# One SBUF region for all loaded tiles, one run a partition for the weights, and V loaded in pairs

## Chip, cores, metric

The kernel runs on one core of one Trainium2 chip. A time is the device time of one execution, in microseconds (us); the smaller, the better. Of a kernel run several times the median is given. The profile is one further execution, recorded by the hardware profiler.

## The reference

One decoding step of a transformer block for 4 sequences (B = 4, D = 576), bfloat16 inputs. An attention with 32 query heads over 16 cached key/value heads (window of 2,048 positions, head width 128) and a mixer with an MLP (F = 4,608) run side by side on the same normed input, and both are added to x:

```python
xn = _layernorm(x)
# attention
q = (xn @ wq)                                   # 4 x 4096, 32 heads
k, v = k_cache[:, :, Sk - W:], v_cache[:, :, Sk - W:]   # W = 2048, each head serves 2 query heads
p = softmax(q k^T * Dh ** -0.5)
a = (p v) @ wo
# mixer and MLP on xn (sequence length 1: the shifted parts are all zeros, so hs = 0)
x1 = xn + hs
h2 = gelu(_layernorm(x1) @ w3) @ w4
out = x + a + x1 + h2
```

The bytes are K and V, 33.6 MB each, wq and wo, 4.7 MB each, w3 and w4, 5.3 MB each: 87 MB read once, for 4 tokens.

## The kernel before

**Loads.** All large loads are issued by SyncE (the SP queue), in the order in which the program names them; a load whose buffer is still in use holds up those behind it. Four buffers of 32 KB a partition (pool `big`, `NBUF = 4`) take K and V in tiles of 4.2 MB: 8 tiles of K, then 8 of V, K0 to K7 and V0 to V7. Each K or V tile has 128 rows of 32,768 contiguous bytes, one to a partition: 32 heads, four quarters of 512 positions. The weights share these buffers. wq comes as four rows a partition (`wq`, 32 KB) and a tail of 64 rows (`wq_t`, in a `kt` buffer); w3 as two rows a partition twice (`w3a`, `w3b`) and a tail; wo as two tiles of 16 rows (`wo0` in a buffer of its own, `wo1`); w4, which is 2 halves of 18 rows a partition, as 11 rows in what is left of the buffer of `w3b`, and after V as 7 + 7 rows in one DMA, 6, 3, and two last rows in two halves of columns (`w_end`). The order of the queue is wq, K0, w3a, K1, w3b with 11 rows of w4, K2 to K7, V0 to V7, wo0, wo1, w_end.

**K stage.** `k_scores(n)` takes a K tile: DVE transposes it in four pieces (L301), PE multiplies the pieces with the queries (L310) and gathers the scores in PSUM banks S. For K5 to K7 DVE also takes the maximum of a bank in between (L287). After K0 and K1 PE runs `g_piece` (L486), xn times w3; after K1 `gelu()` follows on DVE, ACT and PE, and the first 11 rows of w4 are multiplied.

**Between K and V.** The maximum over all scores, four exponentials on ACT (L352), `pick_rows` (8 matmuls, L363) which spreads the probabilities over partitions, `keep_rows` (L368), then `spread_rows(n)`, four DVE operations for each V tile (L381), which writes the weights X.

**V stage.** `v_compute(n)` is 64 matmuls of 128 x 256 (L394). The order of PE, ACT and DVE is that of the program from here on (`manual_schedule`). After V1 PE picks rows for the second half of the heads and turns the reciprocals; after V3 ACT scales the first half (`heads_out(0)`); after V4 `heads_rows(0)` and `heads_pick(0)`, matmuls OX (L424) and three DVE steps (L429 to L433), turn it into the columns `onx` that wo is multiplied with. `v_load(n + 3)` is issued after `v_compute(n)`, when the buffer of V(n - 1) is free.

**The end.** After V7: `heads_out(1)`, `heads_rows(1)`, `heads_pick(1)`, 64 matmuls with wo (`acc_matmuls`, L441), the rest of w4 (`mlp_out`), the sums (`copy_sums`, `merge_sums`), and the last rows of w4 in quarters of columns (`quads`, L455), whose two output copies go to HBM.

Small pieces of SBUF come from `Z`, a tile of 16 KB a partition, through `z_part`.

Of the kernel before, what the change touches and what calls it, by code (L numbers as in the profile page):

```python
# [9 lines left out]
ALU = mybir.AluOpType  # L10
# [5 lines left out]

NBUF = 4
# [3 lines left out]
def kernel(  # L21
# [32 lines left out]
    KJ = 4  # L54
# [3 lines left out]
    DH = D // 2  # L58
    scale = float(Dh) ** -0.5
# [22 lines left out]
    big = ctx.enter_context(tc.tile_pool(name="big", bufs=NBUF))  # L82
    ktp = ctx.enter_context(tc.tile_pool(name="kt", bufs=2))
    pzp = ctx.enter_context(tc.tile_pool(name="pz", bufs=1))
    wop = ctx.enter_context(tc.tile_pool(name="wo", bufs=1))
# [13 lines left out]
    def k_load(bp, kq):  # L99

        t = big.tile([P, CK, Dh], BF16, tag="big", name=f"k{bp}{kq}")
        lo = Sk - W + kq * 4 * CK
        src = k_rows[MT * bp:MT * bp + MT, lo:lo + 4 * CK, :].rearrange("m (q c) d -> m q (c d)", q=4)
        nc.sync.dma_start(out=t[:].rearrange("p c d -> p (c d)"), in_=src)
        return t
# [3 lines left out]
    def v_load(n):  # L109
        bp, kq = V_order[n]  # L110
        t = big.tile([P, CK, Dh], BF16, tag="big", name=f"v{n}")
        lo = Sk - W + kq * 4 * CK
        src = v_rows[MT * bp:MT * bp + MT, lo:lo + 4 * CK, :].rearrange("m (q c) d -> m q (c d)", q=4)
        nc.sync.dma_start(out=t[:].rearrange("p c d -> p (c d)"), in_=src)
        return t

    wq_src = A_wq[0:KJ * P, :].rearrange("(p j) n -> p j n", j=KJ)
    w3_src = B_w3[0:KJ * P, :].rearrange("(p j) f -> p j f", j=KJ)
    w4_src = B_w4.rearrange("(e m i) n -> e m i n", e=2, i=NFH)
    NE0 = 11  # L120
    w4_row = w4_src[0, :, NE0:NFH, :].rearrange("m i n -> m (i n)")
    w4_both = bass.AP(w4_row.tensor, w4_row.offset, [list(w4_row.ap[0]), [(P * NFH - NE0) * D, 2], list(w4_row.ap[1])])
    XR = 16
    NT = Hq * Dh // (P * XR)
    wo_src = A_wo.rearrange("(t p x) n -> p t (x n)", p=P, x=XR)

    JR = 2

    def load_rows(t, a, src, j, n, rows=JR):

        nc.sync.dma_start(out=t[:, a:a + rows * n].rearrange("p (j n) -> p j n", j=rows), in_=src[:, j:j + rows, :])
        return [t[:, a + i * n:a + (i + 1) * n] for i in range(rows)]

    def load_tail(t, a, w, n):
        nc.sync.dma_start(out=t[:, a:a + n // 2], in_=w[KJ * P:D, :].rearrange("r (e f) -> (r e) f", e=2))
        return t[:, a:a + n // 2]

    BIG = CK * Dh


    wq_t = load_tail(ktp.tile([P, NQ // 2], BF16, tag="kt", name="wq_t"), 0, A_wq, NQ)
    wq_m = big.tile([P, BIG], BF16, tag="big", name="wq")
    wq_j = load_rows(wq_m, 0, wq_src, 0, NQ, KJ)
    K_order = [(bp, kq) for bp in range(2) for kq in range(4)]
    V_order = K_order
    K_tiles = {0: k_load(*K_order[0])}
# [26 lines left out]
    def transposed_prep(src_bf, name, pad=0):  # L173
        dup = const.tile([B, 2, P], BF16, name=f"dup_{name}")
        nc.vector.memset(dup[:], 0.0)
        for e in range(2):
            nc.vector.tensor_copy(out=dup[:, e, e:P:2], in_=src_bf[:, KJ * P:D])
        T = const.tile([P, KJ + 2, B + 2 * pad], BF16, name=name)
        if pad:
            nc.vector.memset(T[:], 0.0)  # L180
        return src_bf, dup, T[:, :, pad:pad + B], T

    def transposed_pe(prep):
        src_bf, dup, T, _ = prep
        tp = ps_tp.tile([P, KJ + 2, B], BF16, tag="tp")
        for j in range(KJ):
            nc.tensor.transpose(out=tp[:, j, :], in_=src_bf[:, j:KJ * P:KJ], identity=ident[0:B, 0:B])
        for e in range(2):
            nc.tensor.transpose(out=tp[:, KJ + e, :], in_=dup[:, e, :], identity=ident[0:B, 0:B])
        nc.vector.tensor_copy(out=T, in_=tp[:])  # L190

# [10 lines left out]

    qz = z_part(2 * NM * NY * G, BF16).rearrange("p (a m y n) -> p a m y n", a=2, m=NM, y=NY)

    layernorm(xn_f, xn_bf, x_bf)
    xn_prep = transposed_prep(xn_bf, "xnT", B)
    xnT = xn_prep[3]
# [8 lines left out]
    GP0 = 320  # L218
# [4 lines left out]
    HB = QN // Dh  # L223
    qp = ps_s.tile([P, QN], F32, tag="S", name="qp")
    nc.vector.memset(qp[:], 0.0)
    transposed_pe(xn_prep)

    def q_piece(t, j):
        for n in range(NQ // QN):
            i, k = divmod(n, 2)  # L230
            if j < KJ:
                x, rhs = xnT[:, j, :], t[:, n * QN:(n + 1) * QN]
            else:
                e, f0 = divmod(n * QN, NQ // 2)
                x, rhs = xnT[:, KJ + e, :], t[:, f0:f0 + QN]

            nc.tensor.matmul(out=qp[32 * i:32 * i + 2 * B, :], lhsT=x[:, B - B * k:3 * B - B * k], rhs=rhs,  # L237
                             start=False, stop=False, skip_group_check=True)

    q_piece(wq_t, KJ)  # L240
    for j in range(KJ):
        q_piece(wq_j[j], j)
# [10 lines left out]

    tq = ps_o.tile([P, 2, HB // rep, NY, rep, 4 * B], F32, tag="O", name="tq")
    rows = bass.AP(ident[:].tensor, ident[:].offset, [list(ident[:].ap[0]), [B, 2], [G, 4], [1, B]])
    for y in range(NY):
        for m in range(HB):
            m2, r = divmod(m, rep)
            nc.tensor.matmul(out=tq[:, :, m2, y, r, :].rearrange("p k (i b) -> p k i b", b=B),
                             lhsT=q_rows[:, m, y, :, :].rearrange("p g i -> p (g i)"), rhs=rows,  # L260
                             start=(y + m == 0), stop=(y == NY - 1 and m == HB - 1), skip_group_check=True)
    YM = NY * G
    for g in range(NG):
        g1, g0 = divmod(g, 2)
        for bp in range(2):
            src = ap_part(tq, G * g, G, 2 * g0 * B + 2 * bp + g1,
                          [[rep * 4 * B, 4 * NY], [B, 2], [4 * B, rep]])
            dst = ap_part(qz, G * g, G, bp * NM * YM + 8 * g0 + 4 * bp + 2 * g1,
                          [[G, 4 * NY], [4 * YM + 16, 2], [1, rep]])
            if bp:  # L270
                nc.scalar.copy(out=dst, in_=src)
            else:
                nc.vector.tensor_copy(out=dst, in_=src)
# [3 lines left out]
    ln2T = ln2_prep[2]  # L277
# [11 lines left out]
    def k_scores(n):  # L289

        bp, kq = K_order[n]
        kn = K_tiles.pop(n)
# [31 lines left out]
    sums = z_part(DH, F32)  # L324

# [32 lines left out]
    def pick_rows(bp, g0, g1):  # L358
        for r in range(rep):
            if (bp, r) not in CPS:  # L360
                CPS[bp, r] = ps_s.tile([P, NG * CK], F32, tag="S", name=f"C{bp}{r}")
            for q in range(4):
                nc.tensor.matmul(out=CPS[bp, r][:, g0 * CK:g1 * CK], lhsT=pick[:, bp, r, 3 - q:3 - q + P],  # L363
                                 rhs=EP[:, g0:g1, q, :], start=(q == 0), stop=(q == 3), skip_group_check=True)
# [81 lines left out]
    def load_wo(t, pool, tag):  # L446
        w = pool.tile([P, XR, D], BF16, tag=tag, name=f"wo{t}")
        nc.sync.dma_start(out=w[:].rearrange("p x n -> p (x n)"), in_=wo_src[:, t, :])
        return w

# [18 lines left out]
    NI3 = NFH // 2  # L469
    G_banks = []  # L470

    def g_open():
        for k in range(2):
            bank = ps_o.tile([P, 4 * P], F32, tag="O", name=f"G{k}")
            nc.vector.memset(bank[:], 0.0)
            G_banks.append((bank[:], 4 * k, 4))
        G_banks.append((ACC[:, GP0:GP0 + P], 8, 1))

    def g_piece(t, j):
        w = t if len(t.shape) == 2 else t[:]  # L480
        for bank, i0, n in G_banks:
            for a in range(4):
                e, h = divmod(a, 2)
                lhsT, f0 = (ln2T[:, j, :], e * (F // 2)) if j < KJ else (ln2T[:, KJ + e, :], 0)
                rhs = bass.AP(w.tensor, w.offset + f0 + NI3 * h + i0, [list(w.ap[0]), [1, n], [NFH, P]])
                nc.tensor.matmul(out=bank[32 * a:32 * a + B].rearrange("p (i m) -> p i m", m=P), lhsT=lhsT, rhs=rhs,  # L486
                                 start=False, stop=False, skip_group_check=True)

    def gelu():
        z_at[0] = 2 * NM * NY * G  # L490
        xs = z_part(NI3 * P, F32)
        u = z_part(NI3 * P, F32)
        g = z_part(NI3 * P, BF16)
        for k, (bank, i0, n) in enumerate(G_banks):
            (nc.scalar.copy if k == 1 else nc.vector.tensor_copy)(out=xs[:, i0 * P:(i0 + n) * P], in_=bank)
        nc.vector.tensor_tensor(out=u, in0=xs, in1=xs, op=ALU.mult)
        nc.vector.tensor_scalar(out=u, in0=u, scalar1=GA, scalar2=1.0, op0=ALU.mult, op1=ALU.add)
        nc.vector.tensor_tensor(out=u, in0=u, in1=xs, op=ALU.mult)
        nc.scalar.activation(out=u, in_=u, func=ACT.Tanh, scale=GC)
        nc.vector.tensor_scalar(out=u, in0=u, scalar1=0.5, scalar2=0.5, op0=ALU.mult, op1=ALU.add)  # L500
        nc.vector.tensor_tensor(out=g, in0=u, in1=xs, op=ALU.mult)  # L501
        GT = ps_tp.tile([P, NI3, 4, B], F32, tag="tp", name="GT")
        cols = bass.AP(ident[:].tensor, ident[:].offset, [list(ident[:].ap[0]), [32, 4], [1, B]])
        for i in range(NI3):
# [155 lines left out]
```

## Time and profile before

| | us |
|---|---|
| median of 3 runs | 212.45 |
| the runs | 211.96, 212.45, 212.47 |
| the profiled execution's own time | 211.72 |
| its span in the profile | 209.8 |
| busy in it: PE / DVE / ACT | 120.4 / 134.9 / 15.2 |
| transfers of the SP queue, as a share of 16 DMA engines' span | 97.3% |
| HBM read | 87.17 MB, 416 GB/s over the span |

The span runs from the first to the last instruction; what the program needs around it, 1.9 us here, is in the time alone. PE, PEld (weight loads), DVE (VectorE), ACT (ScalarE) and POOL (GpSimd) are the compute engines, SPq is the queue of SyncE, which issues the loads. Lines such as L394 are those of the kernel's source as printed above. "Idle before" names the wait that ended last before an instruction. A window's line gives its bounds, its length, the busy time of each engine with the number of instructions, the share of TensorE's clock that was granted (PEclk), the share in which the 16 DMA engines were busy, and GB/s. The trace also holds a record for each DMA packet, that is one contiguous run of one partition.

### The profile page before, as it was taken

Reading aid. Unit: us, or ns where it says so; the run is one execution under the profiler, and the core shown is the slowest. Engines: PE = TensorE matmul, PEld = TensorE weight load, DVE = VectorE, ACT = ScalarE, POOL = GpSimd, SP = SyncE. Lnnn points to the kernel's source line nnn. Section 1 sums busy time; section 2 is a strip of 40 time slices with the busy share of each in tenths; the row PEclk is TensorE's granted clock in tenths of the full one; section 3 lists DMA queues with packets and bytes.
Section 4 is the critical chain, followed back from the end, with each engine's and each line's share of the span. In section 5 each row is a group of like instructions: output and inputs, shape, how many; then the busy total and the mean of one; then the engine's idle time right before and its main releaser. Section 6 shows DMA issues by size and latency. Waiting matters only on the chain.

```text
span 209.8 us, 2498 instructions
## 1 busy us (share of the span) xinstructions
PE 120.4 (57%) x1096; PEld 74.9 (36%) x1096; DVE 134.9 (64%) x137; ACT 15.2 (7%) x40; POOL 1.8 (1%) x8
## 2 busy tenths in 40 slices
PE   1434069019145333334444426999799999959562
PEld 0111012002021111111111002887688898848441
DVE  7904792098689898989999614996626848700202
ACT  4002100000200000000000053000200100000101
POOL 2100000000000000000000000000000000000000
PEclk9999557856955555555555555899999999988998
DMA  7999899999999999999999999999999999999992
GB/s 301 400 469 431 381 481 397 424 418 473 439 400 447 437 412 406 481 412 406 472 419 400 469 425 406 462 422 412 456 422 419 444 428 425 409 422 429 411 404 78
DMA packets 4593, 87.31 MB, mean 416 GB/s; under 512 B 476, under 2 KB 1000, under 8 KB 1768
## 3 DMA queue, kind: packets, MB, share of 16 engines
q1 hardware_dynamic: 4568, 87.17, 97.3%
q8 instruction: 8, 0.13, 0.3%
q10 hardware_dynamic: 16, 0.01, 0.0%
q14 instruction: 1, 0.01, 0.0%
HBM read 87.17 MB, written 0.00 MB: 416 GB/s over the span
## 4 chain that ended last, share of the span: by engine, by line
DMA 54%; PE 29%; DVE 11%; ACT 2%; issue 2%; SPq 1%; DVEq 0%; ACTq 0%
DMA k<-in_A_k_cache_dram 41%; PE O L394 21%; DMA w_end<-in_B_w_dram 13%; DVE kt L301 10%; PE G L486 3%; PE C L363 3%; PE S L310 2%; ACT Z L352 1%; DVE mx L287 1%; DVE X L381 1%; ACT Z L368 0%; PE OX L424 0%; SPq L512 0%; PE ACC L486 0%; PE RD L407 0%
## 5 line engine op out<-in xcount | busy, mean ns | idle before, releaser
L301 DVE STREAM_TRANSPOSE kt<-k 128x2048 int32<-128x2048 int32 x32 | 71.4, 2283 | 12.5 <-DMA k<-in_A_k_cache_dram 12.5
L394 PE MATMUL O<-v,X 128*128 128x256 bf16 x512 | 59.5, 281 | 3.9 <-DMA v<-in_A_v_cache_dram 2.3
L310 PE MATMUL S<-kt,Z 128*32 128x512 bf16 x256 | 28.7, 592 | 51.1 <-DVE kt L301 51.1
L394 PEld LDWEIGHTS <-X 128*128 128x128 bf16 x512 | 51.5, 101 | 12.3 <-DVE X L381 2.6
L381 DVE TENSOR_TENSOR X<-Z,own 128x1024 int32<-128x1024 int32 x32 | 37.0, 1220 | 17.9 <-ACT Z L368 6.9
L310 PEld LDWEIGHTS <-Z 128*32 128x32 bf16 x256 | 9.9, 125 | 70.0 <-issue 67.5
L429 DVE TENSOR_TENSOR Z<-OX,own_d 128x512 f32<-128x512 f32 x2 | 1.4, 692 | 18.7 <-PE OX L424 18.7
L363 PE MATMUL C<-Z,pick 128*128 128x512 bf16 x16 | 5.5, 502 | 4.1 <-ACT Z L352 4.1
L352 ACT ACTIVATE Z<-S,nb 128x512 bf16<-128x512 f32 x4 | 2.7, 692 | 64.2 <-DVE nb L562 64.2
L252 DVE CAST q_rows<-qp 128x256 bf16<-128x256 f32 x4 | 1.5, 420 | 7.2 <-PE qp L237 6.5
L486 PE MATMUL G<-w3a,ln2T 128*4 128x512 bf16 x24 | 6.1, 1087 | 0.0
L237 PE MATMUL qp<-wq,xnT 128*8 128x512 bf16 x32 | 3.3, 584 | 3.6 <-DMA wq<-in_A_wq_dram 3.6
L416 ACT ACTIVATE Z<-O,rd_rows 64x128 f32<-64x128 f32 x4 | 1.4, 362 | 46.1 <-PE O L394 46.0
L486 PEld LDWEIGHTS <-ln2T 128*4 128x4 bf16 x60 | 2.1, 107 | 6.8 <-issue 6.4
L363 PEld LDWEIGHTS <-pick 128*128 128x128 bf16 x16 | 1.9, 117 | 7.3 <-issue 6.5
L460 DVE COPY Z<-ACC 64x288 f32<-64x288 f32 x1 | 0.5, 460 | 6.2 <-PE ACC L441 6.2
L505 PE MATMUL GT<-ident,Z 128*128 128x16 bf16 x9 | 0.4, 176 | 7.0 <-DVE Z L501 7.0
L368 ACT CAST Z<-C 128x128 bf16<-128x128 f32 (+2 forms) x6 | 3.0, 544 | 19.7 <-PE C L363 19.7
L486 PE MATMUL G<-w3b,ln2T 128*4 128x512 bf16 x16 | 4.1, 1093 | 0.0
L287 DVE TENSOR_REDUCE mx<-S 128x1 f32<-128x512 f32 x4 | 2.6, 662 | 2.0 <-PE S L310 2.0
L441 PEld LDWEIGHTS <-gT 128*4 128x4 bf16 x62 | 2.3, 96 | 4.4 <-issue 2.6
L237 PEld LDWEIGHTS <-xnT 128*8 128x8 bf16 x40 | 1.2, 111 | 5.7 <-issue 5.3
(95 smaller groups left out, 56.6 us busy)
## 6 DMA issues: line engine op xcount, KB each, us to landing
k<-in_A_k_cache_dram SPq DMA_DIRECT2D x8, 4096.0 KB, 28.7
v<-in_A_v_cache_dram SPq DMA_DIRECT2D x8, 4096.0 KB, 22.0
wo<-in_A_wo_dram SPq DMA_DIRECT2D x2, 2304.0 KB
wq<-in_A_wq_dram SPq DMA_DIRECT2D x1, 4096.0 KB, 12.6
w3a<-in_B_w_dram SPq DMA_DIRECT2D x1, 2304.0 KB, 26.8
w3b<-in_B_w_dram SPq DMA_DIRECT2D x1, 2304.0 KB
w_end<-in_B_w_dram SPq DMA_DIRECT2D x1, 2016.0 KB, 25.1
w3b<-in_B_w_dram SPq DMA_DIRECT2D x1, 1584.0 KB
```

The source lines that it names most:

```text
L237: nc.tensor.matmul(out=qp[32 * i:32 * i + 2 * B, :], lhsT=x[:, B - B * k:3 * B - B * k], rhs=rhs, start=False, stop=False, skip_group_chec ...
L252: nc.vector.tensor_copy(out=dst, in_=src)
L287: nc.vector.reduce_max(out=mx[:, g:g + 1], in_=S[g][:], axis=AX.X)
L301: nc.vector.transpose(out=ap32(kt[e], c0 * 2 * G, [[2 * G, C2 // 2], [1, 2], [2, G]]), in_=ap32(kn, c0 * 4 * G + e * G, [[4 * G, C2 // 2], ...
L310: nc.tensor.matmul(out=S[kq][c:c + 32, :].rearrange("p (c q l) -> p c q l", q=4, l=2), lhsT=qz[:, bp, m, y, :], rhs=kt[e][:, :, 4 * m:4 * ...
L352: nc.scalar.activation(out=EP[:, g].rearrange("p q (c l) -> p c q l", l=2), in_=S[g][:].rearrange("p (c q l) -> p c q l", q=4, l=2), func= ...
L363: nc.tensor.matmul(out=CPS[bp, r][:, g0 * CK:g1 * CK], lhsT=pick[:, bp, r, 3 - q:3 - q + P], rhs=EP[:, g0:g1, q, :], start=(q == 0), stop= ...
L368: nc.scalar.copy(out=CB[:, bp, g0:g1, :, r], in_=CPS[bp, r][:, g0 * CK:g1 * CK].rearrange("p (g c) -> p g c", c=CK))
L381: nc.vector.tensor_tensor(out=ap32(X, a * CX * MT, [[MT, CX], [1, MT]]), in0=bass.AP(s32.tensor, s32.offset, [list(s32.ap[0]), [1, CX], [0 ...
L394: nc.tensor.matmul(out=O_tiles[bp][:], lhsT=X[:, c:c + 2, :].rearrange("p c n -> p (c n)"), rhs=vn[:, c:c + 2, :].rearrange("p c d -> p (c ...
L441: nc.tensor.matmul(out=ACCS[half][o0:o0 + B, 0:DH], lhsT=lhsT, rhs=row[:, q * DH:(q + 1) * DH], start=False, stop=False, skip_group_check= ...
L486: nc.tensor.matmul(out=bank[32 * a:32 * a + B].rearrange("p (i m) -> p i m", m=P), lhsT=lhsT, rhs=rhs, start=False, stop=False, skip_group ...
```

## The change

- One region `ring` of 144,000 bytes a partition replaces the buffers of `big` and `wo`. It has four slots of 32 KB, between the second and the third a gap of 64 elements. K tile n lies in slot n mod 4. Loads wait for whoever reads or writes the bytes that they overwrite.
- wq, w3 and wo are loaded as they lie in HBM, cut into 128 equal runs: 36,864, 41,472 and 36,864 bytes a partition, nine half rows of wq and w3, 32 rows of wo. wq and w3 go to slots 2 and 3 and past them, and both are issued ahead of K0.
- Because a partition now holds half rows, the normed input is transposed into nine slots, each with two groups of columns (`transposed_prep`, `transposed_pe`, `slot_cols`), 20 transposes for 12; q takes 36 matmuls of 512 columns for 40, w3 (`g_all`) 36 of 512 and 18 of 128 for 40 and 20, in one go ahead of the scores of K0.
- V is loaded two tiles at a time, 65,536 bytes a partition, into slots 0 and 1 or 2 and 3: `v_load(0)` and `v_load(2)` ahead of the V stage, `v_load(4)` after V1, `v_load(6)` after V3. `pick_rows` reads the probabilities in the order that goes with it.
- All of w4 comes after V: a half of 18 rows (`w4_e0`), and after wo 7, 6, 3 and the two last rows. The first half and wo lie in slots 0 and 1; 6, 3 and 2 rows lie past slot 3.
- wo in one run makes `XR` 32 and `NT` 1: `heads_rows` has 2 products for 4, and the three DVE steps of `heads_pick` have half the columns.
- GELU: two copies to SBUF on ACT after `g_all`; then, on 640 columns for 1,152, two DVE passes and the tanh after V4, one DVE pass and 5 matmuls for 9 after V5 (`gelu_u`, `gelu_g`, `gelu_T`).
- Some DVE memsets become matmuls with zeros or go to POOL.

The core of the diff:

```diff
-    wq_t = load_tail(ktp.tile([P, NQ // 2], BF16, tag="kt", name="wq_t"), 0, A_wq, NQ)
-    wq_m = big.tile([P, BIG], BF16, tag="big", name="wq")
-    wq_j = load_rows(wq_m, 0, wq_src, 0, NQ, KJ)
-    K_tiles = {0: k_load(*K_order[0])}
+    E1 = (7, 6, 3, 2)
+    GAP = max(0, wo_n + E0_N + E1[0] * D - 2 * TILE)
+    SLOT = [0, TILE, 2 * TILE + GAP, 3 * TILE + GAP]
+    REST = SLOT[3] + TILE
+    ring = ringp.tile([P, RING], BF16, tag="ring", name="ring")
+    def load_run(t, src):
+        nc.sync.dma_start(out=t, in_=src)
+        return t
+    def flat(a, n):
+        return bass.AP(a.tensor, a.offset, [[n, P], [1, n]])
...
+    wq_t = load_run(ring[:, SLOT[2]:SLOT[2] + wq_n], flat(A_wq, wq_n))
+    w3_t = load_run(ring[:, SLOT[2] + wq_n:SLOT[2] + wq_n + w3_n], flat(B_w3, w3_n))
...
     def v_load(n):
         bp, kq = V_order[n]
-        t = big.tile([P, CK, Dh], BF16, tag="big", name=f"v{n}")
+        t = ring[:, SLOT[n % 4]:SLOT[n % 4] + 2 * TILE]
         lo = Sk - W + kq * 4 * CK
-        src = v_rows[MT * bp:MT * bp + MT, lo:lo + 4 * CK, :].rearrange("m (q c) d -> m q (c d)", q=4)
+        src = v_rows[MT * bp:MT * bp + MT, lo:lo + 8 * CK, :].rearrange("m (q c) d -> m q (c d)", q=4)
+        load_run(t, src)
+        for h in range(2):
+            V_tiles[n + h] = t[:, h * TILE:(h + 1) * TILE].rearrange("p (c d) -> p c d", d=Dh)
...
-    XR = 16
+    XR = wo_n // D
...
+    for s in range(NS):
+        for i in range(QI):
+            f0 = s * (NQ // 2) + i * QN
+            nc.tensor.matmul(out=qp[32 * i:32 * i + 2 * B, :], lhsT=slot_cols(xn_prep[1], s), rhs=wq_t[:, f0:f0 + QN], ...)
...
+    g_all()
+    gelu_in()
     for n in range(len(K_order)):
-        if n > 0:
-            K_tiles[n] = k_load(*K_order[n])
...
-    for n in range(NV0):
-        V_tiles[n] = v_load(n)
+    v_load(0)
+    v_load(2)
...
             if n == 4:
                 heads_pick(0, heads_rows(0))
-            if n - 1 + NV0 < NV:
-                V_tiles[n - 1 + NV0] = v_load(n - 1 + NV0)
-            if n == NV - NV0 + 1:
-                wo.append(load_wo(0, wop, "wo"))
-                wo.append(load_wo(1, big, "big"))
...
+                gelu_u()
+            if n == 5:
+                gelu_g()
+                gelu_T()
+            if n % 2 and n + 3 < NV:
+                v_load(n + 3)
+            if n == 5:
+                w4_e0 = load_w4(wo_n, 0, 0, NFH)
+                wo_t = load_run(ring[:, 0:wo_n], flat(A_wo, wo_n))
+                end, i0 = [], 0
+                for k, m in enumerate(E1[:3]):
+                    end.append(load_w4(wo_n + E0_N if k == 0 else REST + (i0 - E1[0]) * D, 1, i0, m))
+                    i0 += m
...
         heads_out(1)
+        mlp_out(*w4_e0)
         heads_pick(1, heads_rows(1))
```

## The prediction

> **What bounds the kernel now.** I read the page first, then windows, the chain, the waits of the SP queue and the timeline of the last 100 us. From the page:
>
> ```profile
> span 209.8 us, 2498 instructions
> ...
> PEclk9999557856955555555555555899999999988998
> DMA  7999899999999999999999999999999999999992
> ...
> q1 hardware_dynamic: 4568, 87.17, 97.3%
> ```
>
> No compute engine is busy for two thirds of the span; the transfers fill it. The windows (busy time of PE, PEld, DVE, ACT, POOL, then clock, DMA share, GB/s) say that they have no hole:
>
> ```profile
> 1.90:206.80 204.90, 120.00 (x1092) 74.73 (x1092) 133.32 (x132) 14.12 (x38) 1.09 (x2) 0.75 1.00 426
> 109.14:187.11 77.97, 62.87 (x525) 49.41 (x525) 49.65 (x46) 7.38 (x19) 0.00 (x0) 0.85 1.00 429
> 184.23:187.64 3.41, 1.12 (x10) 0.82 (x8) 0.00 (x0) 0.00 (x0) 0.00 (x0) 0.97 0.86 369
> 187.64:191.06 3.42, 3.42 (x19) 2.40 (x17) 0.00 (x0) 0.00 (x0) 0.00 (x0) 0.54 1.01 431
> ```
>
> From the first packet (1.9) to the last (206.8) the share is 1.00 (a short window's share errs, as packets are booked at one end). The end of the chain agrees, and the waits of the SP queue show why nothing runs dry: each load waits for its buffer, but behind others still moving.
>
> ```profile
> 179.75 27.26 DMA w_end<-in_B_w_dram
> 207.01 0.04 issue
> 207.05 0.33 PE SUM L455 x4
> ```
>
> ```profile
> SPq L114 <- PE O L394: 41.6, 4, 19.1
> SPq L114 <- DVE kt L301: 36.9, 4, 9.6
> ...
> SPq L599 <- PE O L394: 7.5, 1, 7.5
> ```
>
> So the time is start + (bytes and packets) + 3 us of end, as long as the queue is never empty and PE is ready when the last piece lands. PE's part, in the timeline (start, duration):
>
> ```profile
> 109.42 4.51 DVE L301 STREAM_TRANSPOSE kt<-k 128x2048 int32<-128x2048 int32 x2 [0.32 <-DMA k<-in_A_k_cache_dram]
> 130.13 15.43 PE L394 MATMUL O<-v,X 128*128 128x256 bf16 x128 [1.65 <-DVE X L381]
> 148.83 21.12 PE L394 MATMUL O<-v,X 128*128 128x256 bf16 x192
> 187.11 8.81 PE L394 MATMUL O<-v,X 128*128 128x256 bf16 x64 [2.29 <-DMA v<-in_A_v_cache_dram]
> 196.75 1.16 PE L424 MATMUL OX<-Z 128*128 128x128 f32 x8 [0.83 <-ACT Z L416]
> 197.94 0.69 DVE L429 TENSOR_TENSOR Z<-OX,own_d 128x512 f32<-128x512 f32 x1 [15.44 <-PE OX L424]
> 199.69 2.13 PE L441 MATMUL ACC<-wo,onx 128*4 128x288 bf16 x64 [1.78 <-DVE onx L433]
> ```
>
> The last K tile is taken up at 109.42, the first V tile (64 matmuls) at 130.13; a V tile costs 21.12 / 3 = 7.04 us, or 8.81 where the clock had fallen.
>
> **The change: packets.** The bytes stay. By the shapes (8 partitions to an engine) each of the 16 engines now moves data packets: wq 16, w3 24, K 64, V 64, wo 16, w4 72, so 256, and 28 completions. After: wq 8, w3 8, K 64, V 32, wo 8, w4 64, so 184, and 21 completions. The trace's packet records have these medians: 32,768 B 1216 ns, 18,432 B 689, 4,608 B 178, a completion 9. From 18,432 to 32,768 B, 14,336 B more take 527 ns, 27.2 B/ns, which leaves 11.3 ns a packet; at 4,608 B it leaves 9. 72 packets at 10.4 (between the two, most of them long) and 7 completions at 9 are 0.75 + 0.06 = **0.8 us less**. No packet here is longer than 32,768 B. If every longer run is cut in two (wq 8, w3 8, V 32, wo 8: 56 packets back), 0.2 us is left of it; if a long run lost 1% a byte (18,432 B packets are 0.7% slower a byte than 32,768 B ones), V's 78 us would cost 0.8 more, so the bounds are -0.8 and +0.6. I take -0.8, since the records lie on one straight line.
>
> The Trainium skill (DMA: Bandwidth & Descriptors, Why small descriptors are slow) gives a fixed overhead of about 3 cycles a packet plus 32 B of metadata. At its 850 MHz fabric clock that is an estimated 4.7 ns a packet, by which the sum would be -0.4 and the time 212.1, near the third rival below. The records, at 9 to 11 ns, say twice that.
>
> **Order.** w3 (5.3 MB) goes ahead of K, and the 1.6 MB of w4 that lay ahead go behind V. K0 lands some 12 us later, which costs nothing: its transposes (9 us a tile, a tile each 9.72) follow the transfers anyway. K7 lands earlier by 8 w4 packets x 474 ns = 3.8, and 0.3 of packets: DVE takes it up at 105.35, and with the same 20.7 us of transposes, exponentials and picks V0 starts at 126.1. g_all reads w3 at about 26: 36 + 18 matmuls where 40 + 20 took 10.4 us, done at 36, and K3, which overwrites w3, is due in the queue at 54. Cover 18 us. K2 waits for the q matmuls (17.4) and is due at 45.
>
> The new prep (20 transposes of 4 rows for 12, POOL memsets of 4 partitions for DVE's) ends by about 9, wq lands at 13.7. GELU leaves DVE's K stage: three passes over 640 columns (0.76 us each, from 1.36 for 1,152) and a tanh go into the V stage, where DVE works 50 of 78 us. pick_rows and the scores keep their counts: nothing.
>
> **V in pairs.** The added wait: a pair of V lands as one DMA, and its 64 KB a partition are overwritten as one. SP stops in front of v_load(4) until PE ends V1, of v_load(6) until V3, of w4's first half until V5; the rest of SP's loads are queued behind, and PE waits for those. An issue needs some 1.2 us to its first packet (wq_t issued at 0.73, first packet 1.9). The engines finish K7 spread over 1.9 us (records 107.2 to 109.1), and the last one sets the end. By it, a pair lasts 19.4 us (2 x 9.72 less 8 packets):
> - K7 done at 105.0 on the last engine, V0/1 124.4, V2/3 143.8. V0 and V1 take 15.4 from 126.1: 141.5, first packet 142.7. Slack 1.1 (the earliest engines stand 0.8, which the end does not feel).
> - V2 starts after the picks at 144.8, V3 ends at 159.0; first packet 160.2, needed at 163.1. Slack 2.9.
> - V4/5 at 163.4. PE has stood 4.4 us; the row of 187.11 has 2.3 us of idle, then half a clock for 3.4 us and 8.8 instead of 7.0. So V4 8.8, OX 0.6, V5 7.0: 179.8, first packet 181.0, needed at 182.5. Slack 1.5.
>
> The pairs cost nothing under a cover of 1.1 us at the first place; beyond it, one for one.
>
> **The end.** After the last pair 10 MB remain: 8 x (774 + 1366 + 308 + 266 + 135) ns + 32 x 29 + 0.06 = 23.8 us. PE then has V6 and V7 14.1 (15.9 with a clock drop), heads_out 0.8, the rest of 36 e0 matmuls 0.4, then wo 2.1, 26 matmuls 0.9, copies and merges 1.2. XR becomes 32 and NT 1, so OX goes from 8 to 4 matmuls (0.6) and the three DVE steps from 1.7 to about 1.0. Sum 21.1, or 22.9 cold, against 23.8 + 0.5: PE stays ahead by 1.4, where before it waited three times in the last 5 us.
>
> Sum: 211.72 (profiled: span 209.8 and 1.9 around it) - 0.8 = 210.9. The median of the runs is 212.45, 0.7 above the profiled one, so I predict **211.65** for the median. What a measurement of this kernel can tell from no change is about 0.3%, 0.64 us: the gain stands just past that.
>
> **Rivals.**
> - *The queue runs dry (slower).* PE reaches the end of V1 too late for v_load(4). For it: before, this load waited for one tile only and had 9.7 us more in front of it. Against: it needs V1's end after 142.6, from where each us is lost to the queue; it makes the change slower than before from 143.4, by over 0.3% from 144.0. A stretch of 3.4 us at half clock costs V7 1.77 (8.81 - 7.04). One such stretch more before V1 leaves 0.7 of stall, 212.3; two leave 2.4, **214.1**, which I take for this case.
> - *The tail becomes PE's.* V6 and V7 start together 23.8 us ahead of the end. Past 1.4 us of further delay (a second cold stretch is 1.8) each us counts: 212.0 with one, 213.8 with two.
> - *The packets save less*: the queue cuts long runs, so the change does not do what it says, or a packet costs less than the line through the records has it: 0 to 0.4 saved, 212.2.
>
> The Trainium skill (TensorE: Matmul & The Clock Gate, Part 1: The HAM clock gate) speaks against pairs: after an idle window of about 3.4 us the clock halves. By that rule alone the 4.4 us ahead of V4 would halve it and the 2.9 us ahead of V6 not, and the time would stay 211.65; the row of 187.64 shows it after 2.3 us, which is why I price V6 cold too.
>
> **Chances.** Forecast 0.60: of it 0.47 beyond 0.3%, 0.13 within, since 0.8 is so near 0.64. Dry queue 0.20: 0.15 slower (two stretches), 0.05 within. Tail 0.07: 0.04 slower, 0.03 within. Packets 0.13, within. Faster 0.47, same 0.34, slower 0.19. The runs of before lie 0.5 apart, and long runs may save a little more than the line, so the range begins at 210.8. Above, it goes halfway between one and two cold stretches of the dry queue and the tail, 213.6, which leaves some 0.15 out.
>
> **What would show it.** Right: share 1.00 up to the last packet, packets near 3,300, the chain ending in a DMA, K7's transposes at about 105.3, V0 at 126, the wait of PE for the pair V6/7 near 183. Wrong: a window of share under 0.9 at 142 to 145 or 181 to 184 (dry), a chain ending in PE O, OX and ACC (tail), some 4,200 packets (cut). Above 213.6 the single region's loads wait for more than their own bytes; under 210.8 long runs move faster a byte than any record here.

## The result, and the profile after

| | before | after |
|---|---|---|
| median, us (5 runs each) | 212.1 | 213.71 |
| lowest to highest | 211.75 to 212.47 | 213.19 to 214.14 |
| ratio, 95% interval | | 1.0073, 1.005 to 1.0097 |
| profiled execution: its own time / span | 211.72 / 209.8 | 213.19 / 211.1 |
| last data packet ends, us in the span | 206.57 | 207.96 |

The change makes the kernel slower by 0.7%. The prediction was 211.65 (210.8 to 213.6), most likely faster: the sign was wrong, and the time lies 0.1 above the range.

The page of the changed kernel:

```profile
span 211.1 us, 2458 instructions
...
PEclk9999559955555555555555589996999699969999
DMA  7999999999999999999999999999999999999891
...
q1 hardware_dynamic: 3288, 87.17, 96.7%
```

The packets fell from 4,568 to 3,288 and the bytes stayed, as the change says. In 40 slices the DMA share still looks full. So do windows; but if they are cut by where the pairs of V landed on the last of the 16 engines (their completion records: 124.49, 143.81, 164.32, 184.54), their lengths tell more. Times of packet records are counted from the span's start here, like all others. The prediction has them 0.24 us later (its 206.8 is 206.57), and the windows cut at landings, here and below, begin as much behind them, all alike. Columns as before: bounds, length, busy PE, PEld, DVE, ACT, POOL, then clock, DMA share, GB/s.

```profile
1.90:208.20 206.30, 120.64 (x1081) 73.86 (x1083) 128.73 (x122) 13.94 (x40) 2.62 (x5) 0.75 0.99 422
124.70:144.00 19.30, 16.48 (x140) 13.75 (x140) 17.76 (x18) 2.43 (x6) 0.00 (x0) 0.99 1.04 432
144.05:164.50 20.45, 15.67 (x129) 13.30 (x130) 9.20 (x9) 0.72 (x2) 0.00 (x0) 0.92 0.96 408
164.55:184.75 20.20, 16.26 (x137) 13.73 (x137) 11.09 (x14) 1.03 (x2) 0.00 (x0) 0.92 0.98 419
...
185.00:188.42 3.42, 3.37 (x18) 2.40 (x18) 1.26 (x2) 0.00 (x0) 0.00 (x0) 0.55 1.12 483
```

Rows two to four hold one pair each, of the same 8.4 MB: V2/3 took 19.3 us at 432 GB/s, V4/5 20.5 at 408, V6/7 20.2 at 419. The DMA share only falls from 1.04 to 0.96 and 0.98. The last row is the half clock with which PE begins V6.

The SP queue, start and duration of its issues, shows when the loads of this stretch were let go, and its waits show by whom:

```profile
139.58 0.54 SPq L113 DMA_DIRECT2D ring<-in_A_v_cache_dram  x1
...
160.09 0.53 SPq L113 DMA_DIRECT2D ring<-in_A_v_cache_dram  x1
...
179.08 0.33 SPq L497 DMA_DIRECT2D ring<-in_B_w_dram  x1
```

```profile
SPq L113 <- PE O L383: 30.4, 2, 15.8
...
SPq L497 <- PE O L383: 15.2, 2, 14.4
```

And the timeline, with the lines that answer to those of before (L289 is K7's transposes, L383 the V tiles, L430 wo and w4, L439 the last rows):

```profile
105.73 4.51 DVE L289 STREAM_TRANSPOSE kt<-ring 128x2048 int32<-128x2048 int32 x2 [0.23 <-DMA ring<-in_A_k_cache_dram]
125.40 14.15 PE L383 MATMUL O<-ring,X 128*128 128x256 bf16 x128 [1.66 <-DVE X L370]
164.71 8.54 PE L383 MATMUL O<-ring,X 128*128 128x256 bf16 x64 [4.65 <-DMA ring<-in_A_v_cache_dram]
185.05 15.60 PE L383 MATMUL O<-ring,X 128*128 128x256 bf16 x128 [3.00 <-DMA ring<-in_A_v_cache_dram]
203.74 2.13 PE L430 MATMUL ACC<-ring,onx 128*4 128x288 bf16 x64 [1.25 <-DVE onx L422]
207.63 0.36 PE L439 MATMUL SUM<-ring,gT 128*4 128x144 bf16 x12 [0.49 <-DMA ring<-in_B_w_dram]
```

PE ends V1 at 139.55, 2 us earlier than the prediction had it, and v_load(4) is issued at 139.58. The completion records, one for each of the 16 engines, say that V2/3 landed on the first engine at 141.62 and on the last at 143.81. So the load came 2.0 us before any engine had nothing left. I call this its *lead*: from the issue to the first engine's last completion of what is queued ahead. Even so the pair behind it lost 1.2 us. v_load(6) had a lead of 1.6 (issued 160.09, first engine done at 161.73), and lost 0.9. Together that is 2.1 us on the last engine, and the chain still ends in the transfers:

```profile
139.56 0.02 issue
139.58 25.09 DMA ring<-in_A_v_cache_dram
164.67 0.04 issue
164.71 8.54 PE O L383 x64
...
181.57 26.02 DMA ring<-in_B_w_dram
207.59 0.04 issue
207.63 0.36 PE SUM L439 x12
```

The packet records show where in the pair the time went. They do not name the engine, but a packet that starts 6 ns after a completion record follows it on the same engine. On 12 of the 16 engines the first packet of V4/5 follows so. The other four had V2/3 at 141.62, 141.71, 142.04 and 142.47, and their first packets start at 142.08, 142.38, 142.73 and 143.10: they stood for 0.6 us on average, though the load had long been issued. These four packets took 3.9 to 4.3 us where the median is 2.42, and the engine that began at 143.10 is the one that landed last. In all, of the packets that start between 141.7 and 145, 21 took 2.6 to 4.3 us, 0.9 us for each of the 16 engines; later ones are back at the median but for one. In V6/7 slow packets hold only 0.2 us an engine. There, too, four engines did not go on at once. One of them had V4/5 at 163.35 and began V6/7 only at 165.13; it landed last, together with an engine that stood for 0.9 us in the middle of the pair, as single engines do in every run (see the last section).

### The profile page after: what moved, and what is told of

The parts are those of the page before. It is cut to its first block, busy times and chain, and to the rows that moved or that the text cites. A ratio compares the mean times of both kernels' runs of the same rounds, so it can differ in the third digit from the quotient of the medians.

```text
span 211.1 us, 2458 instructions
## 1 busy us (share of the span) xinstructions
PE 121.1 (57%) x1085; PEld 73.9 (35%) x1086; DVE 130.2 (62%) x125; ACT 15.1 (7%) x42; POOL 4.0 (2%) x10
## 3 DMA queue, kind: packets, MB, share of 16 engines
q1 hardware_dynamic: 3288, 87.17, 96.7%
## 4 chain that ended last, share of the span: by engine, by line
DMA 65%; PE 21%; DVE 9%; issue 1%; ACT 1%; SPq 1%; DVEq 0%; ACTq 0%
DMA ring<-in_A_k_cache_dram 29%; DMA ring<-in_B_w_dram 24%; PE O L383 14%; DMA ring<-in_A_v_cache_dram 12%; DVE kt L289 8%; PE G L465 4%; PE C L352 2%; PE S L298 1%; ACT Z L341 1%; DVE mx L275 1%; DVE X L370 1%; SPq L497 0%; PE SUM L439 0%; PE OX L413 0%; SPq L113 0%
## 5 line engine op out<-in xcount | busy, mean ns | idle before, releaser
L289 DVE STREAM_TRANSPOSE kt<-ring 128x2048 int32<-128x2048 int32 x32 | 71.4, 2283 | 18.5 <-DMA ring<-in_A_k_cache_dram 18.4
L383 PE MATMUL O<-ring,X 128*128 128x256 bf16 x512 | 61.0, 284 | 10.7 <-DMA ring<-in_A_v_cache_dram 9.1
L298 PE MATMUL S<-kt,Z 128*32 128x512 bf16 x256 | 30.4, 622 | 49.6 <-DVE kt L289 49.6
L383 PEld LDWEIGHTS <-X 128*128 128x128 bf16 x512 | 51.9, 102 | 19.6 <-issue 7.9
L418 DVE TENSOR_TENSOR Z<-OX,own_d 128x256 f32<-128x256 f32 x2 | 0.8, 425 | 25.3 <-PE OX L413 25.3
L465 PE MATMUL G<-ring,ln2T 128*8 128x512 bf16 (+1 forms) x54 | 10.4, 860 | 2.3 <-DMA ring<-in_B_w_dram 2.3
L199 PE MATMUL tp<-ident,Z 4*128 4x4 bf16 x20 | 1.1, 164 | 8.8 <-DVE Z L190 8.8
L465 PEld LDWEIGHTS <-ln2T 128*8 128x8 bf16 x54 | 1.9, 97 | 12.0 <-issue 11.1
L230 PE MATMUL qp<-ring,xnT 128*8 128x512 bf16 x36 | 3.5, 562 | 1.2 <-DMA ring<-in_A_wq_dram 1.2
L430 PE MATMUL ACC<-ring,onx 128*4 128x288 bf16 x64 | 2.1, 286 | 1.2 <-DVE onx L422 1.2
L430 PE MATMUL ACC<-ring,gT 128*4 128x288 bf16 x62 | 2.5, 286 | 0.2 <-DMA ring<-in_B_w_dram 0.2
```

The source lines that it names most:

```text
L199: nc.tensor.transpose(out=tp[:, 2 * (NO - 1 - o) + e, :], in_=dup[:, e, o, :], identity=ident[0:B, 0:B])
L230: nc.tensor.matmul(out=qp[32 * i:32 * i + 2 * B, :], lhsT=slot_cols(xn_prep[1], s), rhs=wq_t[:, f0:f0 + QN], start=False, stop=False, skip ...
L289: nc.vector.transpose(out=ap32(kt[e], c0 * 2 * G, [[2 * G, C2 // 2], [1, 2], [2, G]]), in_=ap32(kn, c0 * 4 * G + e * G, [[4 * G, C2 // 2], ...
L298: nc.tensor.matmul(out=S[kq][c:c + 32, :].rearrange("p (c q l) -> p c q l", q=4, l=2), lhsT=qz[:, bp, m, y, :], rhs=kt[e][:, :, 4 * m:4 * ...
L383: nc.tensor.matmul(out=O_tiles[bp][:], lhsT=X[:, c:c + 2, :].rearrange("p c n -> p (c n)"), rhs=vn[:, c:c + 2, :].rearrange("p c d -> p (c ...
L430: nc.tensor.matmul(out=ACCS[half][o0:o0 + B, 0:DH], lhsT=lhsT, rhs=row[:, q * DH:(q + 1) * DH], start=False, stop=False, skip_group_check= ...
```

## The experiments

Theory A: a load that comes late, even one that comes before the queue is empty, runs its first packets slowly, and the pairs make two loads late. Theory B: it is the long run itself (65,536 bytes a partition), or the one DMA of 8.4 MB, whenever it is issued. Theory C: it is neither, and PE's work behind the last pair sets the time.

**e1_halves: a pair as two DMAs, each waiting for its own tile.**

```diff
-        load_run(t, src)
+        for h in (0, 1):
+            load_run(t[:, h * TILE:(h + 1) * TILE], src[:, :, h * TILE:(h + 1) * TILE])
```

> A pair of V is loaded as two DMAs of 32,768 B a partition, each waiting for its own tile alone (V4 for V0, V5 for V1); everything else as in the changed kernel. Theory A (late issue: a load that reaches the queue less than some 3 us before it empties costs about 1 us, whatever the length of its runs): the loads come 7 us earlier, the slow packets at 142 to 145 and 162 to 166 go, 2.0 us come back, 32 packets and 4 completions cost 0.4 again: 213.7 - 2.0 + 0.4 = 212.1, level with the kernel before. Theory B (runs of 65,536 B are what is slow there): the same 212.1, so this run alone does not tell them apart. Theory C (neither; the tail on PE sets the time): 213.7.

Measured: 211.64 us (12 runs), ratio to before 0.9981 (0.997 to 0.9991). The loss is gone. The load of V4 needs only V0's end, that of V5 only V1's, and so on. Windows cut at the landings of V3, V5 and V7 (143.71, 163.08, 182.48), and the wait of PE ahead of V7:

```profile
143.95:163.30 19.35, 19.07 (x174) 17.05 (x175) 10.99 (x10) 1.11 (x4) 0.00 (x0) 1.00 1.00 433
163.30:182.70 19.40, 17.45 (x162) 15.32 (x161) 12.83 (x15) 1.03 (x2) 0.00 (x0) 1.00 0.99 425
```

```profile
183.00 7.15 PE L387 MATMUL O<-ring,X 128*128 128x256 bf16 x64 [1.17 <-DMA ring<-in_A_v_cache_dram]
```

V4 is issued at 134.46 here, with a lead of 7.1, and both pairs of tiles take 19.4 us. PE's clock stays full in both windows, since it stands 1.2 us where it stood 4.65 and 3.00. The last packet ends at 205.91. But e1 changed both the lateness and the length of the run, so B is not out yet; C, which had 213.7 for it, is.

**e2_late_halves: the same short runs, but late.** The second tile of a pair goes first, so that both DMAs wait for V1 (and V3).

```diff
-            for h in (0, 1):
+            for h in (1, 0):
```

> The same two DMAs of 32,768 B a partition, in the other order: the second tile's first, so that the pair is still issued only when PE has left V1 (V3). Theory A (late issue): the loss stays, 213.7 + 0.4 for the packets = 214.1, slow packets again right after 142 and 162. Theory B (long runs): no run is longer than 32,768 B, so the loss goes: 212.1. Theory C (tail): 213.7 to 214.

Measured: 214.32 (6 runs), ratio 1.0096 (1.0064 to 1.0128), 0.6 us above the changed kernel. Its runs lie between 213.05 and 215.26, the profiled one is at 215.0. Windows cut at the landings (143.69, 163.71, 184.42):

```profile
143.95:163.95 20.00, 16.02 (x129) 13.46 (x129) 8.79 (x9) 0.73 (x2) 0.00 (x0) 0.91 0.99 414
163.95:184.65 20.70, 16.53 (x137) 13.93 (x137) 12.12 (x14) 1.03 (x2) 0.00 (x0) 0.92 0.98 416
```

With packets of 32,768 bytes the first late tile took 10.34 us on the last engine where an undisturbed one takes 9.7, the second 10.97 (from 163.71 to 174.68). Both landed last on an engine that had stood for at least 1.1 us before its first packet. So short runs lose too, and B falls: the DMAs are halves and the time is lost all the same. From the last piece of w4's first half (190.56) to the last packet (209.26) this run also took 18.7 us, 1.4 more than the changed kernel (190.68 to 207.96): three engines ended 0.8 to 1.7 us behind the other 13. I did not find why.

**e3_mix: pairs in one run where nothing waits (V0 to V3), single tiles from V4 on.**

```diff
-        load_run(t, src)
+        if n >= 4:
+            for h in (0, 1):
+                load_run(t[:, h * TILE:(h + 1) * TILE], src[:, :, h * TILE:(h + 1) * TILE])
+        else:
+            load_run(t, src)
```

> V0 to V3 as pairs of 65,536 B a partition, V4 to V7 as single tiles of 32,768 B with waits of their own. Theory A: no load is late, half of the packets stay saved: 212.1 - 0.2 = 211.9, 0.1% under the kernel before. Theory B: the long runs of V0 to V3 cost what the others did, about 1 us a pair: 213.9. Theory C: 213.7.

Measured: 211.38 (11 runs), ratio 0.9967 (0.9956 to 0.9979): it beats both kernels, and its median is the lowest one here, though its interval overlaps that of e1. Long runs by themselves cost nothing. From K7 to V3 on the last engine it took 38.64 us (105.08 to 143.73), e1 38.81: 0.17 saved by 16 packets and 2 completions. Its profiled execution was the slowest of its runs (211.91), and there PE, not the transfers, ended last. The wait ahead of wo:

```profile
200.00 4.01 PE L434 MATMUL ACC<-ring,onx 128*4 128x288 bf16 x64 [8.00 <-DMA ring<-in_A_wo_dram]
```

PE is now so early that it stands 8 us for wo; the 64 matmuls then run 4.01 us, where they took 2.13 before.

**e4_rows_ahead: the pairs as changed, but 1.6 MB of w4 queued behind V2/3.** The 6, the 3 and the 2 last rows of w4 go to bytes that no tile uses. They are loaded after `v_load(2)`, and give v_load(4) and v_load(6) more lead without any earlier issue.

```diff
     v_load(2)
+    end, i0 = [], E1[0]
+    for m in E1[1:3]:
+        end.append(load_w4(REST + (i0 - E1[0]) * D, 1, i0, m))
+        i0 += m
+    last = ring[:, REST + (i0 - E1[0]) * D:REST + (NFH - E1[0]) * D].rearrange("p (i n) -> p i n", n=D)
+    (its two loads by halves of the columns, too; both leave their place after V5)
```

> The pairs of 65,536 B as in the changed kernel, but the 6, 3 and 2 last rows of w4 (1.6 MB, their bytes are free since w3 is used) are issued behind V2/V3, ahead of V4/V5, so the queue holds 3.8 us more when V4/V5 is issued. The last piece to land is then the 7 rows. Theory A: the DMA share is 1.00 and the packets 2.42 us at the transitions into V4/V5 and V6/V7; the last pair lands at about 186.5 (3.8 later, 2.0 won), and PE's 23 us behind it set the end: 214.5 to 215. Theory B: slow packets at both transitions as before, the last pair at 188.5, 216.5 or more.

Measured: 213.57 (4 runs), ratio 1.008 (1.0058 to 1.0103); I had expected about 1 us more. v_load(4) was issued at 139.74, as late as in the changed kernel, but with a lead of 5.9, v_load(6) with 4.6. No first packet of these pairs took more than 2.49 us: V4/5 and V6/7 took 19.4 us (147.77 to 167.15) and 19.3 (to 186.48), and the last packet ended at 205.93, 2.0 us earlier than in the changed kernel. That is A's mechanism: the lead, not the time of issue. Still the time hardly fell, for the last pair now lands 4.0 us later than in e1, behind the rows, at 186.48 for 182.48:

```profile
186.94 14.13 PE L383 MATMUL O<-ring,X 128*128 128x256 bf16 x128 [1.24 <-DMA ring<-in_A_v_cache_dram]
```

PE then ends the matmuls of wo at 206.30, just as the last piece is there (206.31). That piece is now the 7 rows of w4 and no longer the 2, so 26 matmuls, the copies and the sums come behind it, 2.7 us in all. The two causes, the late pair and the order of the rows, were not tested apart. So a pair is bound from two sides: the load must come early enough for the queue, and must land early enough for two tiles of PE work. One load of this run speaks against a fixed bound for all loads: w4's first half was issued at 182.72, 1.6 us before the first engine had V6/7 (184.33), and lost nothing. Its first packets took 0.8 to 1.2 us for 0.77 on the four earliest engines, and none of them stood.

**f3_three_rows: only the 3 rows of w4 (1.1 us of the queue) behind V2/3.** This asks how much lead is enough.

```diff
     v_load(2)
+    three = load_w4(REST + E1[1] * D, 1, E1[0] + E1[1], E1[2])
...
-                    end.append(load_w4(...))
+                    end.append(three if k == 2 else load_w4(...))
```

> The pairs of the changed kernel, with three rows of w4 (3,456 B a partition, 1.1 us of queue) behind V2/V3. Theory A: V4/V5 is issued 3.4 us ahead of the empty queue instead of 2.3 and loses next to nothing (0.1 for 1.1); V6/V7 is issued 2.0 to 2.3 ahead and loses 0.7 to 1.1 still. One of the two losses comes back, but the last pair has 1.1 us more ahead of it, so it lands at 184.9 as in the changed kernel, and PE's work behind it keeps the time at 213.3 to 213.7. Theory B (long runs): losses of 1 us at both places.

Measured: 213.23 (4 runs), ratio 1.0053 (1.004 to 1.0066). One of the two losses was won back, the other stayed:

```profile
145.20:164.60 19.40, 15.18 (x127) 12.85 (x126) 8.81 (x8) 0.72 (x2) 0.00 (x0) 0.94 1.02 430
164.65:185.05 20.40, 16.43 (x137) 13.88 (x137) 11.28 (x14) 1.03 (x2) 0.00 (x0) 0.92 0.96 409
```

Cut at the landings (144.96, 164.38, 184.82), the first window is V4/5, whose load had a lead of 2.8, the second V6/7, whose lead was still 1.6. At V6/7 no engine stood for more than 0.1 us; here the loss is in first packets of up to 4.1 us alone. Leads and losses, the loss on the last engine against 19.3 us a pair, 9.7 a tile or 6.15 for the first half of w4:

| load | lead, us | loss, us |
|---|---|---|
| e2, V6/7 | 1.5 | 1.3 |
| f3, V6/7 | 1.6 | 1.1 |
| e4, first half of w4 | 1.6 | 0.0 |
| changed, V6/7 | 1.6 | 0.9 |
| e2, V4/5 | 2.0 | 0.7 |
| changed, V4/5 | 2.0 | 1.2 |
| changed, first half of w4 | 2.7 | 0.0 |
| f3, V4/5 | 2.8 | 0.1 |
| e4, V6/7 | 4.6 | 0.0 |
| e4, V4/5 | 5.9 | 0.1 |
| e1, V4 | 7.1 | 0.0 |

A load of V with a lead of 2.0 us or less lost about 1 us each time, from 2.8 on next to nothing. Other loads lost less: besides the row of e4, wq at the start of the kernel before (lead 2.1) and the second part of wq in f2 (2.4) lost 0.1 us at most. What makes the difference was not tested.

**f1_wo_first and f2_small_start: can e3 be bettered?** f1 is e3 with wo loaded ahead of w4's first half, against the 8 us of waiting (its 36 matmuls then come behind wo). f2 is f1 with wq in two DMAs, the first with 4,096 bytes a partition as before, against the 0.2 to 0.3 us that the start of the queue had lost.

```diff
-                w4_e0 = load_w4(wo_n, 0, 0, NFH)
                 wo_t = load_run(ring[:, 0:wo_n], flat(A_wo, wo_n))
+                w4_e0 = load_w4(wo_n, 0, 0, NFH)
...
-        mlp_out(*w4_e0)
         heads_pick(1, heads_rows(1))
...
-        for part in end[:2]:
+        for part in [w4_e0] + end[:2]:
```

> V0 to V3 as pairs, V4 to V7 as single tiles, and wo issued ahead of w4's first half, whose 36 matmuls come behind the 64 of wo. In the run with the mix alone PE stood 8 us for wo (landing at 199.96), at a clock that had fallen, and its 64 + 26 matmuls then ended 0.7 us behind the last piece. Theory A with the tail: wo lands at 194, behind which only 36 + 26 matmuls are left, so the end is the last piece again: 211.4 - 0.5 = 210.9. If the end was not PE's: 211.4.

```diff
-    wq_t = load_run(ring[:, SLOT[2]:SLOT[2] + wq_n], flat(A_wq, wq_n))
+    wq_t = ring[:, SLOT[2]:SLOT[2] + wq_n]
+    for c0, c1 in ((0, 2048), (2048, wq_n)):
+        load_run(wq_t[:, c0:c1], flat(A_wq, wq_n)[:, c0:c1])
```

> As the run with wo first, and wq in two DMAs, the first of 4,096 B a partition. In the changed kernel the first packet on each engine is one of 36,864 B and takes 0.3 to 1.0 us more than its 1.36, in the kernel before the first are of 4,096 B and 0.1 to 0.4 more. If what a start costs goes with the size of the first packets: wq lands 0.3 earlier, all behind it too, less 0.1 for 8 packets and a completion: 0.2 under the run with wo first. If a start costs what it costs: 0.1 more than it.

Measured: f1 211.78 (12 runs), ratio 0.9979 (0.9968 to 0.999); f2 212.12 (11 runs), ratio 0.9996 (0.9983 to 1.0008). Both miss. In f1 the wait ahead of wo shrank as meant,

```profile
193.90 3.38 PE L434 MATMUL ACC<-ring,onx 128*4 128x288 bf16 x64 [2.17 <-DMA ring<-in_A_wo_dram]
```

but the last packet ended at 205.99 (e3: 205.97), and its interval overlaps that of e3: that the wait was a bound is not shown. In f2 wq landed at 13.30 to 14.15, as without the split (13.42 to 14.15 in f1), so the length of the first run is not what costs it. What does stays open.

## Why the prediction was wrong, step by step

- **Packets (-0.8): right.** Runs of 65,536 bytes go as one packet of 2,418 ns, 41,472 bytes take 1,533, 36,864 take 1,364; the changed kernel has 3,288 packets in the queue ("near 3,300"). e1 (V in single tiles: 32 packets and 4 completions an engine back, so -0.4 by the same working) measured -0.47 against before's 212.11, and e3 (16 and 2 back, -0.6) measured -0.73. The rival that the queue cuts long runs is out. So is the lower price per packet that came from the Trainium skill (DMA: Bandwidth & Descriptors, Why small descriptors are slow): the step from 32,768 bytes (1,213 ns) to 65,536 leaves 8 ns a packet, nearer to the records' 9 to 11 than to the 4.7 estimated from the page.
- **Order: right, but for the start.** K7 was taken up at 105.73 (105.35 predicted), V0 began at 125.40 (126.1), V0/1 landed at 124.49 (124.4 in the prediction's count, 124.2 in this one), V2/3 at 143.81 (143.8, so 143.6). The first 36,864-byte packets took 1.4 to 2.4 us instead of 1.36, and wq landed on the last engine at 14.14, before at 13.50: a loss that no term held, of which some 0.2 us is left at V2/3.
- **V in pairs: the step that failed**, in its sentence "An issue needs some 1.2 us to its first packet", from which it put the pairs at nothing; they cost 2.1 us. The wait was named right, and so were who waits for what and when it matters. The size of the lead was wrong, and with it the remark that the end does not feel when the earliest engines stand: V4/5 landed last on an engine that had had V2/3 at least 1.3 us before the last one did, then stood and had a first packet of 4.3 us. The 1.2 us (1.0 in the profile's count: wq_t's first packet starts at 1.76) is what the first load of the program needs, into an empty queue; it says when a first packet moves, not how early a load must come for the queue to keep its rate. For the loads of V that takes more than 2.0 us, and 2.8 was enough (table above). By the prediction's own times, with engines that finish 1.9 us apart and in the profile's count, v_load(4) had a lead of 0.2 (V1's end at 141.5, the first engine done at 141.7), v_load(6) 2.0 (159.0, 161.0) and w4's first half 0.6 (179.8, 180.4): with the table the two pairs would have cost some 2 us, not nothing. In fact PE was 2 us earlier at V1, which left 2.0, by luck; at V3 it was 1.1 later, since it stood ahead of V2, too, and V2 began cold (8.46 us), a stretch that no step priced; and w4's first half kept 2.7, because it overwrites only a part of the slot of V5 and was let go at 179.08, before V5's end. The trace of before has no load of V that comes so near to the end of its queue (the least lead is 7.3: V4, issued at 138.60, and the first engine had V3 at 145.90). That missing row should have had a bound of its own in the sum and the range.
- **Dry queue (rival, 0.20): the right place, the wrong mechanism.** It put the loss at v_load(4) after V1, but from the point at which the queue is empty (V1's end past 142.6) and through two stretches of half clock. V1 ended at 139.55 with no such stretch, and the four engines that ran empty did so with the load already issued. Its time, 214.1, was near for another reason. The sign that it named, a share under 0.9 at 142 to 145, wasn't there: such a short window reads 1.10, and one at 181 to 184, where nothing was lost, 0.73. The landings of the tiles show the loss.
- **The end: right.** PE met the last piece with waits of 0.24 and 0.49 us, and V6 and V7 took 15.60 cold (15.9 priced), V4 8.54 (8.8). The tail as a rival needs later loads: e4 comes to it, where PE ends wo only as the last piece lands.
- **The clock: right for V4 and V6.** After 3.00 us of waiting V6 began with a granted clock of 0.55 over the next 3.42 us. The Trainium skill (TensorE: Matmul & The Clock Gate, Part 1: The HAM clock gate) puts that at an idle window of about 3.4 us; this trace has it after 3.0, and that of before after 2.3.

The sum again, to the last packet: 206.57 - 0.8 = 205.8; plus 0.2 (to V2/3), 1.2 (V4/5), 0.9 (V6/7), less 0.1 (what remains) is 208.0, as measured (207.96). The last four terms are read from the trace that they explain; what tests them are e1, e4 and f3, in which the losses went as the leads grew.

The Trainium skill (DMA: Bandwidth & Descriptors, Rules for kernel authors) advises to coalesce many small transfers into one large one. The tiles of V, 4.2 MB each, are not small, and for them the runs show both: a gain where the load is early (e3, 0.17 us for two pairs), a loss where merging makes it late. e3 and the changed kernel differ in the pairs V4/5 and V6/7 alone, and there the coalesced form is slower, 213.71 us for 211.38.

## What to carry to other kernels

In a kernel bound by its transfers, ask of every load that waits for a buffer how far ahead of the end of its queue it is issued; here each load of V with 2.0 us or less of queued work ahead cost about 1 us, and with 2.8 next to nothing, though the DMA share still read 0.96 to 0.98. That is no bound for all loads: one of w4 lost nothing with 1.6. Longer runs save what the packet records say (8 to 11 ns a packet), but a tile that is twice as large comes free later and lands later: merge the loads that wait for nothing, and leave the others small. Time equal loads by their landings: that shows a loss of 5 to 6% which the DMA share hides.

## What was not expected of the hardware

- A load of V issued 1.5 to 2.0 us before the first engine is empty does not reach all engines in time: in V4/5 four of the 16 stood for 0.6 us on average, in V6/7 again four, one of them for 1.8 us, and first packets took up to 4.3 us for 2.42. In f3 (V6/7, 1.6) none stood for more than 0.1 us, and the first packets alone were slow. Engines that still had work were slowed as well (their packets that started up to 144.9 by 0.3 to 0.5 us). Why is open.
- In every run, that of before too, one engine at a time stands for about 1 us, and its next packet mostly takes 0.5 us more: in the kernel before at 138.85, 154.40, 169.01 and 182.45, in the changed one at 154.95 and 175.86. The cause is open.
- A run of 65,536 bytes is one packet at 27.1 bytes a ns, no slower a byte than 32,768 (27.0).
- The first load of a program pays too: 36,864-byte packets took up to 1 us more than later ones, and splitting off a small first run (f2) changed nothing.
